# Sixteen rows of V instead of eight straight into the result, and a shorter serial stretch, at the end of a one-token attention kernel

## The chip, the cores and the metric

One core of one Trainium2 chip. The metric is the device time of one execution in microseconds (us), median of several executions. An execution's time is about 1.7 us longer than the span of its trace, so spans are compared with spans and times with times. The "granted clock" below is the share of TensorE's full clock that the trace shows: 1.00 is full, 0.50 half.

## The reference

```python
# q: [8, 32, 1, 128], k and v: [8, 32, 4096, 128], bf16
scores = jnp.einsum('bhqd,bhkd->bhqk', q, k) * 128 ** -0.5
attn = softmax(scores, axis=-1)
return jnp.einsum('bhqk,bhkd->bhqd', attn, v)
```

256 heads, one query each: every byte of K and V (537 MB) is read once.

## The kernel before

32 tiles of 8 heads. In a tile each of the 128 partitions holds C = 256 rows of 128 numbers ("row" below is one of these 256). VectorE and TensorE make the scores, ScalarE the weights `w`, TensorE the weighted sum of V. For the last three tiles four rows at a time are multiplied (a 128x512 matmul with 32 columns of weights), and the matmuls are dealt to four column groups of the array; each group sums into its own 32 partitions of `av` (these are the "value matmuls", and together the "value sum"). A copy to `comb` and four small matmuls with `pick` (the "sums over groups") bring these together in `op`; ScalarE scales `op` and stores it. The last rows of the last tile skip `av`: their weights, laid out in `w_last`, multiply V straight into `op` ("direct" matmuls, 128x128, 16 columns). The last V tile is loaded in seven pieces.

```python
LAST = 8
...
        ("v", NT - 1): [C // 2, C // 4, C // 8, C // 16, C // 32, LAST // 2, LAST // 2],
...
    def values_of(t, lo, hi):                      # cut
        end = C if t < NT - 1 else C - LAST
        group = [
            0 if t == NT - 1 and C // 2 <= c0 < C // 2 + 3 * C // 16 else c0 // CB % TG
            for c0 in range(0, end, CB)
        ]
        for c0 in range(lo, hi, CB):
            i = c0 // CB
            j = group[i]
            nc.tensor.matmul(                                                    # L322
                avs[t][j * AG : (j + 1) * AG, :], lhsT=w[:, i, :, :],
                rhs=vt[:, c0 : c0 + CB, :], start=(i < TG), stop=(j not in group[i + 1 :]),
            )
...
    def result_of(t):                              # cut; the copy to comb is L351
        if t == NT - 1:
            for i in range(LAST):
                nc.tensor.matmul(                                                # L361, direct
                    ops[n][:], lhsT=w_last[:, i, :], rhs=loads["v", t][:, C - LAST + i, :],
                    start=False, stop=False,
                )
        e = AG if t < LT else P
        for m in range(CB):
            nc.tensor.matmul(                                                    # L367, sum over groups
                ops[n][:], lhsT=pick[0:e, m, r, :], rhs=comb[0:e, m, :],
                start=(r == 0 and m == 0), stop=(r == R - 1 and m == CB - 1),
            )
...
        values_of(NT - 1, 0, C // 2)               # the end of the program
        norm_of(NQ - 1)
        recip_of(NQ - 1)
        values_of(NT - 1, C // 2, C - LAST)
        copy_of(NT - 1)
        result_of(NT - 1)
        finish_of(NQ - 1)                          # scaling, L376
        store_of(NQ - 1)
```

Of the kernel before, what the change touches and what calls it, by code (L numbers as in the profile page):

```python
# [15 lines left out]
TG = 4  # L16
R = 2
OB = 4
LAST = 8
LOOP = 6  # L20
EDGE = 2
NEG = -1.0e30
# [3 lines left out]
def kernel(  # L26
# [10 lines left out]
    P = nc.NUM_PARTITIONS  # L37
# [3 lines left out]
    C = S // PH  # L41
    NT = NH // G
# [4 lines left out]
    CB = 4  # L47
# [3 lines left out]
    AG = CB * G  # L51
    NV = C // CB
    assert (NV - 2 * EDGE) % LOOP == 0
    assert LAST % CB == 0 and TG * AG == P and NH % P == 0 and P % G == 0 and TB % PH == 0 and C % CB == 0

# [73 lines left out]

    w_last = consts.tile([P, LAST, RG], BF16, name="w_last")  # L130
    nc.gpsimd.memset(w_last[:], 0.0)
# [4 lines left out]
    def behind_loop(made):  # L136
# [10 lines left out]
        ("k", 0): [C // 4, C // 4, C // 2],  # L147
        ("k", NT - 2): [C // 2] * 2,
        ("k", NT - 1): [C // 4, C // 4, C // 2],
        ("v", NT - 1): [C // 2, C // 4, C // 8, C // 16, C // 32, LAST // 2, LAST // 2],  # L150
    }

    def load(kind, t):
# [78 lines left out]
    def weights_of(t):  # L232
# [26 lines left out]
        if t == NT - 1:  # L259
            for i in range(LAST // CB):  # L260
                nc.gpsimd.tensor_copy(
                    out=w_last[:, i * CB : (i + 1) * CB, RG - G : RG].rearrange("p m g -> p g m"),
                    in_=w[:, (C - LAST) // CB + i, :, :],
                )
# [40 lines left out]
    LT = NT - 3  # L305

    def values_of(t, lo, hi):
        vt = loads["v", t]
        w = ws[t]
        if lo == 0:  # L310
            avs[t] = ps_v.tile([P, CB * D], F32, name="av", tag="av")
        end = C if t < NT - 1 else C - LAST


        group = [
            0 if t == NT - 1 and C // 2 <= c0 < C // 2 + 3 * C // 16 else c0 // CB % TG
            for c0 in range(0, end, CB)
        ]
        for c0 in range(lo, hi, CB):
# [6 lines that stand above are left out]
# [28 lines left out]
    def result_of(t):  # L354
        n, r = divmod(t, R)
        comb = combs.pop(t)
        if r == 0:
            ops[n] = ps_o.tile([RG, D], F32, name="op", tag="op")
        if t == NT - 1:
            for i in range(LAST):  # L360
                nc.tensor.matmul(  # L361
                    ops[n][:], lhsT=w_last[:, i, :], rhs=loads["v", t][:, C - LAST + i, :],
                    start=False, stop=False,
                )
        e = AG if t < LT else P
        for m in range(CB):
            nc.tensor.matmul(  # L367
                ops[n][:], lhsT=pick[0:e, m, r, :], rhs=comb[0:e, m, :],
                start=(r == 0 and m == 0), stop=(r == R - 1 and m == CB - 1),
            )  # L370

    def finish_of(n):
        s, u = divmod(n, OB)
        if u == 0:
            stages[s] = o_pool.tile([RG, OB, D], BF16, name="stage", tag="stage")
        made = nc.scalar.activation(  # L376
            out=stages[s][:, u, :], in_=ops.pop(n)[:], func=ACT.Copy, scale=rzs.pop(n)[:, 0:1]
        )
        behind_loop(made)
# [12 lines left out]
    with tc.manual_schedule(engines={E.PE, E.DVE, E.Activation, E.SP}):  # L392
        q_prep(0)
        q_prep(1)
        for t in range(NT):
# [10 lines left out]
            if 0 < t - 1 <= LT:  # L406
                if (t - 1) % R == 0:
                    norm_of(n)
                if t > 1:
                    result_of(t - 2)  # L410
# [23 lines left out]
            if v_last:  # L434
                values_of(t - 1, 0, C)
# [4 lines left out]
            if t > 0:  # L440
                copy_of(t - 1)
                if t > 2 and t % R == 1:
                    store_of(n)
                if not loop:
                    if t % R == 0:
                        norm_of(n)
                    result_of(t - 1)
        values_of(NT - 1, 0, C // 2)
# [5 lines that stand above are left out]
        finish_of(NQ - 1)  # L454
        store_of(NQ - 1)
# [30 lines left out]
```

## Time and profile before

| | before |
|---|---|
| time, three runs | 1251.53, 1251.85, 1252.07 us |
| the execution whose trace was taken | 1252.91 us, span 1251.1 |
| HBM read | 536.94 MB, 429 GB/s over the span |
| busy: TensorE, VectorE, ScalarE | 63%, 82%, 13% |

The transfers are the bound until about 5 us before the end (39 of the page's 40 slices have the DMA engines busy for 90% or more, and the last piece of V lands at 1246.34 of 1251.1); what follows is the tail. The lines that carry this stand in the prediction.

### The profile page before, as it was taken

To read this page: it belongs to the slowest core of one execution; us is meant where nothing else is said; L and a number is where in the kernel's file an instruction comes from. 1 tells how busy PE (TensorE), PEld (TensorE's weight loads), DVE (VectorE), ACT (ScalarE), POOL (GpSimd) and SP (SyncE) were. 2 spreads that over 40 slices of the span, in tenths; PEclk is the share of its full clock that TensorE was granted. 3 is DMA by queue.
4 is the path that set the end of the run, shared out by engine and by line. 5 is a ranking of instruction groups with operands and counts; after the bars stand their busy time and mean duration, and the time that the engine had idled before them with its cause. 6 is when DMAs were issued, how large, how long until landed. Compare 5 with 4: busy or idle time off the path is not lost. (4 is left out here: it accounts for less than half of the span.)

```text
span 1251.1 us, 10828 instructions
## 1 busy us (share of the span) xinstructions
PE 794.4 (63%) x3110; PEld 301.4 (24%) x3110; DVE 1021.8 (82%) x495; ACT 166.1 (13%) x433; POOL 4.1 (0%) x22
## 2 busy tenths in 40 slices
PE   2466567655576655766557765577665776657756
PEld 0122122222232222322222222222222222212212
DVE  6977887878977789777798777987779877798783
ACT  0111011111011110111101111011110111101111
POOL 1000000000000000000000000000000000000000
PEclk9687788777887778877788877887877878779866
DMA  9999999999999999999999999999999999999997
GB/s 404 436 436 434 436 436 432 434 436 432 432 426 430 437 434 434 430 430 436 436 436 434 434 434 432 432 430 436 434 432 432 430 435 436 436 434 418 430 437 318
DMA packets 11432, 537.33 MB, mean 429 GB/s; under 512 B 1808, under 2 KB 2064, under 8 KB 2320
## 3 DMA queue, kind: packets, MB, share of 16 engines
q1 hardware_dynamic: 11072, 536.94, 99.4%
q8 instruction: 15, 0.25, 0.1%
q10 hardware_dynamic: 336, 0.07, 0.0%
q14 instruction: 9, 0.07, 0.0%
HBM read 536.94 MB, written 0.07 MB: 429 GB/s over the span
## 5 line engine op out<-in xcount | busy, mean ns | idle before, releaser
L191 DVE TENSOR_TENSOR kt<-kt,qb 128x8192 bf16<-128x8192 bf16 (+1 forms) x99 | 560.8, 5665 | 146.7 <-DMA kt<-in_k_dram 139.7
L211 PE MATMUL ps<-kt,ident 128*128 128x512 bf16 x800 | 284.1, 519 | 383.5 <-DVE kt L199 295.2
L294 PE MATMUL av<-vt,w 128*32 x1740 | 425.1, 396 | 4.6
L194 DVE TENSOR_TENSOR kt<-kt 128x4096 bf16<-128x4096 bf16 (+1 forms) x99 | 288.8, 2917 | 3.4
L294 PEld LDWEIGHTS av<-vt,w 128*32 x1740 | 173.0, 99 | 262.4 <-issue 120.1
L211 PEld LDWEIGHTS <-ident 128*128 128x128 bf16 x800 | 97.0, 121 | 563.9 <-issue 530.0
L223 DVE TENSOR_REDUCE sc<-ps 128x64 f32<-128x512 f32 x128 | 85.3, 685 | 53.4 <-PE ps L211 53.4
L248 ACT ACTIVATE e<-sc,nmax 128x256 bf16<-128x256 f32 x32 | 16.2, 508 | 705.9 <-DVE nmax L242 705.9
L255 ACT ACTIVATE w<-e,mine 128x256 bf16<-128x256 bf16 x256 | 105.6, 495 | 1.1
L199 DVE TENSOR_TENSOR kt<-kt 128x2048 bf16<-128x2048 bf16 x56 | 68.6, 1225 | 1.9
L351 ACT ACTIVATE comb<-av 32x512 bf16<-32x512 f32 (+1 forms) x32 | 18.8, 587 | 331.0 <-PEq L284 321.2
L280 PE MATMUL av<-vt,w 128*32 128x512 bf16 x116 | 47.1, 498 | 14.7 <-issue 13.2
L367 PE MATMUL op<-comb,pick 32*16 32x128 bf16 (+1 forms) x128 | 12.1, 213 | 22.1 <-ACT comb L351 22.1
L280 PEld LDWEIGHTS av<-vt,w 128*32 128x32 bf16 x116 | 6.9, 100 | 55.0 <-issue 55.0
L177 PE MATMUL qp<-qg,heads 8*128 8x128 bf16 x32 | 6.9, 216 | 16.8 <-ACT qg L175 16.8
L322 PE MATMUL av<-vt,w 128*32 128x512 bf16 x190 | 16.5, 425 | 0.7 <-DMA vt<-in_v_dram 0.7
L367 PEld LDWEIGHTS <-pick 32*16 32x16 bf16 (+1 forms) x128 | 8.7, 83 | 29.2 <-issue 28.8
L235 DVE TENSOR_REDUCE pmax<-sc 128x1 f32<-128x256 f32 x32 | 13.4, 420 | 1.1
L175 ACT ACTIVATE qg<-qh 8x128 bf16<-8x128 f32 x32 | 8.5, 267 | 33.7 <-PE qh L171 33.7
L171 PE MATMUL qh<-q_all,ident 128*8 128x128 bf16 x32 | 7.1, 223 | 8.9 <-DMA q_all<-in_q_dram 8.6
L179 ACT ACTIVATE qb<-qp 128x128 bf16<-128x128 f32 x32 | 8.9, 278 | 9.7 <-PE qp L177 9.7
L322 PEld LDWEIGHTS <-w 128*32 128x32 bf16 x190 | 6.9, 104 | 9.8 <-issue 5.8
(31 smaller groups left out, 48.1 us busy)
## 6 DMA issues: line engine op xcount, KB each, us to landing
kt<-in_k_dram SPq DMA_DIRECT2D x4, 4096.0 KB, 24.4
kt<-in_k_dram SPq DMA_DIRECT2D x4, 2048.0 KB, 13.4
vt<-in_v_dram SPq DMA_DIRECT2D x1, 4096.0 KB, 34.9
vt<-in_v_dram SPq DMA_DIRECT2D x1, 2048.0 KB, 39.4
vt<-in_v_dram SPq DMA_DIRECT2D x1, 1024.0 KB, 41.5
vt<-in_v_dram SPq DMA_DIRECT2D x1, 512.0 KB, 42.2
vt<-in_v_dram SPq DMA_DIRECT2D x31, 25.9
kt<-in_k_dram SPq DMA_DIRECT2D x29, 28.4
```

Of the source, the lines that this page charges most:

```text
L191: nc.vector.tensor_tensor(out=part, in0=part, in1=qb[:].to_broadcast([P, hi - lo, D]), op=ALU.mult)
L194: nc.vector.tensor_tensor(out=part[:, :, 0 : D // 2], in0=part[:, :, 0 : D // 2], in1=part[:, :, D // 2 : D], op=ALU.add,)
L199: nc.vector.tensor_tensor(out=part[:, :, 0 : D // 4], in0=part[:, :, 0 : D // 4], in1=part[:, :, D // 4 : D // 2], op=ALU.add,)
L211: nc.tensor.matmul(ps[:], lhsT=ident[:], rhs=kt[:, u * UC : (u + 1) * UC, s * DS : (s + 1) * DS], start=(s == 0), stop=(s == n - 1),)
L223: made = nc.vector.tensor_reduce(out=scs[t][:, u * UC : (u + 1) * UC], in_=sums.pop((t, u))[:], axis=AX.X, op=ALU.add)
L248: nc.scalar.activation(out=e[:], in_=sc[:], func=ACT.Exp, bias=nmax[:, 0:1], scale=scale, accum_out=esums[t // R][:, t % R : t % R + 1],)
L255: nc.scalar.activation(out=w[:, :, g, :], in_=e_g, func=ACT.Copy, scale=mine[:, 0, g : g + 1])
L280: pe.matmul(av, lhsT=wf[:, i * nw : (i + 1) * nw], rhs=vf[:, i * nv : (i + 1) * nv], **how)
L294: pe.matmul(av, lhsT=wf[:, bass.ds(ow + i * nw, nw)], rhs=vf[:, bass.ds(ov + i * nv, nv)], start=False, stop=False,)
L322: nc.tensor.matmul(avs[t][j * AG : (j + 1) * AG, :], lhsT=w[:, i, :, :], rhs=vt[:, c0 : c0 + CB, :], start=(i < TG), stop=(j not in group[ ...
L351: nc.scalar.activation(out=comb[0:n, :, :], in_=av[0:n, :, :], func=ACT.Copy)
L367: nc.tensor.matmul(ops[n][:], lhsT=pick[0:e, m, r, :], rhs=comb[0:e, m, :], start=(r == 0 and m == 0), stop=(r == R - 1 and m == CB - 1),)
```

## The change

Two edits. Rows 240-247 become direct too (16 direct rows instead of 8; the pieces of the load keep their sizes, 8, 4 and 4 rows, only their names change), and the last four direct matmuls go behind the sums over groups, so that they need not wait for the last piece before those. And only 24 rather than 48 rows, from row 128 on, are put in column group 0 alone.

```diff
-LAST = 8
+LAST = 16
@@
-        ("v", NT - 1): [C // 2, C // 4, C // 8, C // 16, C // 32, LAST // 2, LAST // 2],
+        ("v", NT - 1): [C // 2, C // 4, C // 8, C // 16, LAST // 2, LAST // 4, LAST // 4],
@@
-            0 if t == NT - 1 and C // 2 <= c0 < C // 2 + 3 * C // 16 else c0 // CB % TG
+            0 if t == NT - 1 and C // 2 <= c0 < C // 2 + 3 * C // 32 else c0 // CB % TG
@@ result_of (cut)
+        def last_rows(lo, hi):
+            for i in range(lo, hi):
+                nc.tensor.matmul(
+                    ops[n][:], lhsT=w_last[:, i, :], rhs=loads["v", t][:, C - LAST + i, :],
+                    start=False, stop=(i == LAST - 1),
+                )
+        if t == NT - 1:
+            last_rows(0, 3 * LAST // 4)
         for m in range(CB):
             nc.tensor.matmul(
                 ops[n][:], lhsT=pick[0:e, m, r, :], rhs=comb[0:e, m, :],
-                start=(r == 0 and m == 0), stop=(r == R - 1 and m == CB - 1),
+                start=(r == 0 and m == 0), stop=(r == R - 1 and m == CB - 1 and t < NT - 1),
             )
+        if t == NT - 1:
+            last_rows(3 * LAST // 4, LAST)
```

More of the change, by code (lines that the diff above doesn't have):

```diff
@@ L358, in result_of @@
             ops[n] = ps_o.tile([RG, D], F32, name="op", tag="op")
-        if t == NT - 1:
-            for i in range(LAST):
+        e = AG if t < LT else P
+        def last_rows(lo, hi):
+            for i in range(lo, hi):
                 nc.tensor.matmul(
                     ops[n][:], lhsT=w_last[:, i, :], rhs=loads["v", t][:, C - LAST + i, :],
-                    start=False, stop=False,
+                    start=False, stop=(i == LAST - 1),
                 )
-        e = AG if t < LT else P
+        if t == NT - 1:
+            last_rows(0, 3 * LAST // 4)
         for m in range(CB):
```

## The prediction

What no trace or run shows is cut from the text, and each cut is marked. Its sum comes to -1.07 us (scaling at 1247.36 instead of 1248.43), and the step of 1.0 behind 1250.85 is worked out from the trace of before. The 0.427, 0.218 and 0.056 us are times from start to start in that trace: 128x512 at half clock, 128x512 at full clock, 128x128 at full clock. That group 0 is a queue is read from those starts and the order of the program; the trace does not name a matmul's group.

> **What bounds the kernel now.** I read the page first (which resource is full), then the chain of waits that ended last (where the end is set), then the landings of the last V tile and the order of time over the last ten microseconds.
>
> The page:
>
> ```profile
> DMA  9999999999999999999999999999999999999997
> GB/s 404 436 436 434 436 436 432 434 436 432 432 426 430 437 434 434 430 430 436 436 436 434 434 434 432 432 430 436 434 432 432 430 435 436 436 434 418 430 437 318
> HBM read 536.94 MB, written 0.07 MB: 429 GB/s over the span
> ```
>
> Thirty-nine of forty slices are full of transfers at about 434 GB/s; only the last slice (31.3 us) falls, to 318. The change moves no byte, so it can only win in that tail. The chain that ended last shows the tail as links:
>
> ```profile
> 1201.87 39.43 DMA vt<-in_v_dram
> 1241.30 0.04 issue
> 1241.35 5.93 PE av L322 x26
> 1247.28 0.02 issue
> 1247.30 0.02 ACTq L351
> 1247.32 0.04 issue
> 1247.36 0.61 ACT comb L351
> 1247.97 0.04 issue
> 1248.01 0.40 PE op L367 x4
> 1248.41 0.02 issue
> 1248.43 0.36 ACT stage L376
> ```
>
> Up to 1241.30 the end waits for a V piece (rows 128 to 191 of each partition's 256; a "row" below is one of these 256); from then on for TensorE, then copy, sum over groups, scaling, store. The question is whether those 5.93 us of TensorE are held by data or by TensorE. The DMA view of the tail has issue to landing:
>
> ```profile
> vt<-in_v_dram SPq DMA_DIRECT2D x1, 1024.0 KB, 41.5
> vt<-in_v_dram SPq DMA_DIRECT2D x1, 512.0 KB, 42.2
> vt<-in_v_dram SPq DMA_DIRECT2D x1, 256.0 KB, 42.4
> vt<-in_v_dram SPq DMA_DIRECT2D x2, 128.0 KB, 29.2
> ```
>
> The issues start, by the order of time of the queue, at 1202.35, 1202.83, 1203.30, 1207.35 and 1226.69, so the pieces land at about: rows 192-223 at 1243.8, 224-239 at 1245.0, 240-247 at 1245.7, 248-251 at 1246.0, 252-255 at 1246.3 (the view of V's tile gives 19.6 us as the shortest landing, hence 1226.69 + 19.6 for the last, and 2 x 29.2 - 19.6 = 38.8 us for the other). The last value matmul starts at 1246.9, 1.2 us after its data. So TensorE is late, not the data, by about 0.9 us at the end. Busy time of TensorE in the throttle's own steps:
>
> ```profile
> 1238.76:1242.17 3.41, 2.70 (x24) 0.50 0.99 403
> 1242.17:1245.58 3.41, 3.41 (x16) 0.50 0.51 196
> 1245.58:1249.00 3.42, 2.50 (x33) 1.00 0.03 7
> ```
>
> (columns: length, TensorE busy, its matmuls, granted clock, DMA share, GB/s). The clock is half until 1245.58. And in the order of time the pace shows in the weight loads:
>
> ```profile
> 1244.71 0.15 PEld L322 LDWEIGHTS <-w 128*32 128x32 bf16 x1 [0.28 <-issue]
> 1245.14 0.15 PEld L322 LDWEIGHTS <-w 128*32 128x32 bf16 x4 [0.28 <-issue]
> 1245.57 1.19 PEld L322 LDWEIGHTS <-w 128*32 128x32 bf16 x16 [0.28 <-issue]
> 1247.09 0.61 PE L361 MATMUL op<-vt,w_last 128*16 128x128 bf16 x8
> ```
>
> From 1241.35 nine matmuls go one by one, 0.427 us apart; from 1245.14 four at a time. In the program 12 rounds (48 rows) are put in column group 0 alone, and of the 30 matmuls after 1241.35 group 0 gets 12 + 5 = 17, the other groups 5, 4 and 4. 17 explains the starts: ten at half clock, 1241.35 + 0.38 + 8 x 0.427 = 1245.14, one more step of 0.427 to 1245.57, then six steps of (1246.9 - 1245.57)/6 = 0.218 at full clock. Group 0 is thus a queue that never runs dry, and it alone ends the value sum; the other groups finish beside it.
>
> [...] 0.427 and 0.218 us, 0.056 us for the eight small ones ((0.61 - 0.219)/7), and the clock changes at the end of the window 1242.17 to 1245.58, the first after the wait that is wholly busy. [...] the program's last value matmul is in group 1, yet the one that starts last, at 1246.9, is by the count above group 0's 17th. [...] the copy starts 0.11 us after group 0's end (1246.875 + 0.379 = 1247.25). [...]
>
> **The change part by part.** The pieces keep their sizes (8, 4, 4 rows are now called LAST/2, LAST/4, LAST/4), so DMA is unchanged; comparing instruction order on each engine shows no move before the last tile. POOL makes four small copies of weights rather than two; the two took 0.46 us and were done at 1237.4, so four end near 1237.7, eight microseconds before use. Cost nil.
>
> *Removed:* the two value matmuls of rows 240-247, one of them group 0's last. *Moved:* rows 152-175 (six matmuls) are dealt to all groups. Group 0 now gets 6 + 5 = 11 matmuls: six alone (rows 128-148), then rows 160, 176, 192, 208, 224. The others get 5, 6 and 6. Group 0 keeps its pace: 11th start at 1241.35 + 0.38 + 9 x 0.427 = 1245.57. Do the waits hold? Its 9th (row 192) would start at 1244.71, data 1243.8; its 11th (row 224), data 1245.0. Both in time, the latter by 0.5 us. So its last start goes from 1246.88 to 1245.57, that is 6 x 0.218 = 1.31 us earlier. The end of the value sum is 1245.57 + 0.39 = 1245.96; the copy starts 0.11 later, 1246.07, takes 0.60, and the sum over groups may start 0.05 after it: 1246.71 instead of 1248.01.
>
> *Added beside:* twelve direct matmuls (rows 240-251), full clock by then. Eight from 1245.80 at 0.056: to 1246.24 (data 1245.7); four more to 1246.47 (data 1246.0). All under the copy, 0.24 us before it ends: nothing on the path.
>
> *Added on the path:* the four for rows 252-255 behind the four sums over groups: 4 x 0.056 = 0.22 us. Their data, 1246.3, is there before the sums start at 1246.71. So the last of eight starts at 1246.71 + 7 x 0.056 = 1247.10 and the scaling starts 0.256 later (as 1248.173 to 1248.429 now), at 1247.36 instead of 1248.43.
>
> Scaling, store and the closing semaphores (1248.43 to 1251.12, 2.69 us) are the same. Sum: -1.31 + 0.01 (a matmul across the clock's step) + 0.22 = -1.07 us in an execution with this clock phase: span 1250.0.
>
> **The clock's phase.** [...] I let its boundary B fall elsewhere. Before, with 17 x 0.427 = 7.25 us of cold work, half of what is left at B is saved: the value sum ends at about B + (7.25 - (B - 1241.35))/2. B = 1244.8: scaling starts near 1247.9 before, and 1247.0 after (now the landings at 1245.7 and 1246.0 hold the direct rows), gain 0.8. B = 1246.5: 1248.7 and 1247.6, gain 1.1. B = 1247.5: 1249.2 and 1248.1, gain 1.1. I take 1.0: 1251.85 - 1.0 = 1250.85.
>
> **Rivals.** (a) *A bigger gain*, 6 x 0.427 = 2.6 us, if the six serial matmuls counted at their cold length. Against: the last six steps of the queue are the warm ones, and ending earlier forgoes exactly those; besides, data land up to 1246.3. About 1249.3 even so. (b) *The clock stays at half.* [...] Against: group 0 alone still runs from 1241.35 to 1245.96, beyond 1245.58. (c) *A data wait replaces the queue.* If the last piece landed over 0.6 us later than here, the four matmuls behind would wait for it; a later landing of rows 224-239 moves everything. The end would gain less, some 0.5 us: 1251.3. (d) *All hidden, nothing gained*, as the load bounds the kernel: refuted by the 0.9 us between last landing and last value matmul's end.
>
> **Range and chances.** The three runs of before spread over 0.54 us, which the clock's phase alone can make, and the landings move with every execution. With a step of 1.0 from a 1251.85 base I take 1249.9 to 1251.7 for 8 in 10. Two per cent are 25 us; the whole tail behind the last landing is 4.8 us, so neither side is reachable by this change; 0.005 each for something unseen.
>
> **What would show it.** Right: L322 has 28 matmuls after the wait, singles for about 2.6 us less; the copy starts near 1246.1 (with full clock from about 1245.6) or 4.7 us after the wait's end; sixteen direct matmuls, twelve ending before the copy does; the scaling about 6.0 us after the wait's end, against 7.08 now. Wrong: an idle gap of TensorE with a V landing as its end ahead of row 224 or behind the sums; the clock at half beyond 1247; or the copy starting later than 0.11 us after group 0's last matmul.

## The result, and the profile after

1251.43 us median (1251.33 to 1251.86, 6 runs), against 1251.95 us (1251.53 to 1252.26, 6 runs) for the kernel before: 0.52 us. The ratio is 0.9997 with a 95% interval of 0.9984 to 1.001 (the ratios given here are not quite those of the medians quoted). The interval is 1.6 us wide to each side, more than any effect, so the gain in time is by itself not clear of noise; small differences are therefore read from the traces, and times are used where whole sets of runs stand apart.

Predicted was 1250.85, with 1249.9 to 1251.7 as range. The time is within it, and "within 2%" is right, but the gain is half of the 1.0 us predicted, and the range, 1.8 us wide, was met without the step that was to bring the gain, as the trace shows.

The trace after is from an execution of 1251.86 us, span 1250.2. The end of its chain of waits (start, length, what):

```profile
1204.55 41.43 DMA vt<-in_v_dram
1245.98 0.04 issue
1246.02 0.83 PE op L363 x12
1246.85 0.22 PE op L371 x4
1247.08 0.24 PE op L363 x4
1247.31 0.02 issue
1247.34 0.36 ACT stage L382
```

Before, the chain left the load at 1241.30, with the landing of rows 128-191, and spent 5.93 us in TensorE's value matmuls. Now it stays in the load until 1245.98: the issue at 1204.55 plus 41.43 us is the landing of rows 240-247 (the 256 KB piece). Behind it there are only the twelve direct matmuls, the sums, and the four direct ones. The copy is no link any more. The order of time shows what the value matmuls did meanwhile (in brackets: TensorE idle before, and what ended it):

```profile
1241.62 1.89 PE L322 MATMUL av<-vt,w 128*32 128x512 bf16 x16 [1.09 <-DMA vt<-in_v_dram]
...
1244.14 0.61 PE L322 MATMUL av<-vt,w 128*32 128x512 bf16 x8 [0.63 <-DMA vt<-in_v_dram]
...
1245.37 0.40 PE L322 MATMUL av<-vt,w 128*32 128x512 bf16 x4 [0.62 <-DMA vt<-in_v_dram]
...
1245.88 0.60 ACT L351 ACTIVATE comb<-av 128x512 bf16<-128x512 f32 x1 [7.59 <-PE av L322]
1246.02 0.83 PE L363 MATMUL op<-vt,w_last 128*16 128x128 bf16 x12 [0.25 <-DMA vt<-in_v_dram]
```

TensorE waits for each piece: 0.63, 0.62 and 0.25 us. The prediction had it late throughout. The reason is one column of the "windows", the stretches of 3.41 us at whose ends the granted clock changes in these traces (in the trace of before it falls at 675.56 and at 1238.76, 165 stretches of 3.413 us apart, and is back to full at 1245.58, two later). Here they are in the trace of after (length, TensorE busy, matmuls, clock, DMA share, GB/s):

```profile
1237.19:1240.60 3.41, 2.19 (x40) 1.00 0.96 405
1240.60:1244.01 3.41, 1.89 (x16) 1.00 0.87 344
1244.01:1247.43 3.42, 2.29 (x32) 1.00 0.21 76
```

The clock is full when rows 128-191 land; in the trace of before it was half until 1245.58. The program is the same up to there but for two more small copies on POOL, so the change did not cause this; *before_again* below shows the kernel before with full clock too. Two traces that differ in the clock cannot be subtracted: that scaling now starts at 1247.34 rather than 1248.43 is 1.09 us, almost exactly the predicted 1.07; the agreement is luck, for the larger part is not the change's doing.

### The profile page after: what moved, and what is told of

Same layout as the page of the kernel before. It is cut to its first block, busy times and chain, and to the rows that moved or that the text cites. A ratio compares the mean times of both kernels' runs of the same rounds, so it can differ in the third digit from the quotient of the medians. Undisturbed runs are those within 1.5% of the kernel's fastest.

```text
span 1250.2 us, 10842 instructions
## 1 busy us (share of the span) xinstructions
PE 786.8 (63%) x3116; PEld 299.6 (24%) x3116; DVE 1021.9 (82%) x495; ACT 166.1 (13%) x433; POOL 4.5 (0%) x24
## 5 line engine op out<-in xcount | busy, mean ns | idle before, releaser
L211 PE MATMUL ps<-kt,ident 128*128 128x512 bf16 x800 | 278.4, 511 | 389.9 <-DVE kt L199 299.7
L280 PE MATMUL av<-vt,w 128*32 128x512 bf16 x116 | 47.2, 499 | 14.6 <-issue 13.1
L322 PE MATMUL av<-vt,w 128*32 128x512 bf16 x188 | 13.7, 418 | 2.3 <-DMA vt<-in_v_dram 2.3
L237 DVE TENSOR_SCALAR spread<-same,pmax 128x32 f32<-128x32 f32 x32 | 7.7, 242 | 1.1
```

The source lines that it names most:

```text
L211: nc.tensor.matmul(ps[:], lhsT=ident[:], rhs=kt[:, u * UC : (u + 1) * UC, s * DS : (s + 1) * DS], start=(s == 0), stop=(s == n - 1),)
L280: pe.matmul(av, lhsT=wf[:, i * nw : (i + 1) * nw], rhs=vf[:, i * nv : (i + 1) * nv], **how)
L322: nc.tensor.matmul(avs[t][j * AG : (j + 1) * AG, :], lhsT=w[:, i, :, :], rhs=vt[:, c0 : c0 + CB, :], start=(i < TG), stop=(j not in group[ ...
```

## The experiments

Twelve runs. For each trace three things are compared: the clock at the landing of rows 128-191, and how long scaling starts after the last V piece (rows 252-255) and after rows 240-247 have landed. These delays do not depend on when the load ends, which moves by 0.4 us between executions. For the trace of before they are 2.09 and 2.76 us, for that of after 0.69 and 1.36; a table has them all. "Runs of before" are those made beside, on the same chip. Each expectation weighs two readings. The "clock theory" has the gain depend on whether the clock is half or full when rows 128-191 land; "corrected theory" adds that ordinary executions have full clock there.

**Full or half clock forced in both kernels.** For full clock, ten spare matmuls behind the second-last tile, where TensorE idled (cut; the 10 is written in):

```diff
+    def filler(n):
+        kt = loads["k", NT - 1]
+        ps = ps_s.tile([P, UC, DS], F32, name="fill", tag="ps")
+        for i in range(n):
+            nc.tensor.matmul(
+                ps[:], lhsT=ident[:], rhs=kt[:, 0:UC, 0:DS], start=(i == 0), stop=(i == n - 1)
+            )
@@
                 values_of(t - 1, 0, C)
+                if t == NT - 1:
+                    filler(10)
```

For half clock, 28 of the 32 matmuls of the last tile's first half left out; the result is then wrong (relative error 0.10):

```diff
         for c0 in range(lo, hi, CB):
             i = c0 // CB
+            if t == NT - 1 and TG <= i < C // 2 // CB:
+                continue
```

*before_warm*, the kernel before with the spare matmuls:

> The kernel before, with ten spare matmuls (128x512, 0.216 us each at full clock) on TensorE behind the second-last tile, where it idled for 2.5 us in the trace of before. Clock theory [...] the clock is full from about 1235 to the end, group 0's queue of 17 keeps up, and the tail is held by landings. From the landings of before, rows 240-247 at 1245.67: copy at about 1246.2, scaling 1247.3, about 0.9 us behind the last V landing (2.1 us behind it in the trace of before); time 0.5 to 1.0 us under before. Rival (landings come later in the changed kernel, clock is beside the point): time as before, 1251.95.

Measured: 1251.83 us (1251.74 to 1252.04), runs of before 1251.74 (1251.51 to 1252.03), ratio 1.0001 (0.9987 to 1.0015). Full clock from 1232.12 on; scaling 0.94 us after the last landing. The state of the tail was as expected, the time was not: the kernel before is not slower than its own copy with the clock held at full. So its ordinary runs lose nothing to the clock, and the traced one of 1252.91 us was the exception.

*after_warm*, the changed kernel with the same spare matmuls:

> The changed kernel with the same ten spare matmuls. Clock theory: full clock as in its own profile; scaling starts about 0.7 us behind the last V landing; only 0.2 to 0.3 us faster than the kernel before with the spare matmuls, since both wait for the same landings; and about as fast as the changed kernel's best (1251.3). Rival that the change itself costs or gains a fixed amount whatever the clock: the gap between the two is the 0.52 us of the pair without spare matmuls.

Measured: 1251.50 us (1251.41 to 1251.60), ratio to before 0.9998 (0.9984 to 1.0012). Scaling 0.70 us after the last landing. All five runs lie under all five of *before_warm*; the gap of the medians is 0.33 us, just above the expected 0.2 to 0.3.

*before_cold* and *after_cold*, with the 28 matmuls left out:

> The kernel before without 28 of the 32 matmuls of the first half of the last V tile (the result is wrong on purpose): TensorE idles from about 1235 to 1241.3 but for a few short ones. Clock theory: the clock is half when rows 128-191 land in every execution, group 0 has ten or so steps of 0.427 us, scaling starts 6.5 to 8.2 us after that landing (7.1 in the trace of before); time at or up to 0.5 us above before. Rival: time as before.

> The changed kernel with the same matmuls left out (wrong on purpose). Clock theory: half clock at the landing as above, group 0's 11 steps at 0.427 us, copy about 4.7 us after the landing, scaling 5.7 to 7.0 us after it; 0.8 to 1.1 us faster than the kernel before with the same left out. That is the step of 1.0 that I predicted for every execution. Rival (fixed amount): 0.52 us between the two.

Measured: *before_cold* 1252.53 us (1252.30 to 1253.38), ratio 1.0008 (0.9994 to 1.0022); *after_cold* 1251.58 us (1251.46 to 1252.29), ratio 1.0000 (0.9987 to 1.0014). The gap is 0.95 us; the two sets of runs do not overlap, though by 0.01 us only. Scaling 6.70 and 5.70 us after rows 128-191 landed. With half clock at that landing the change is worth about what I predicted for every execution, with full clock a third of that; a fixed 0.52 us fits neither gap. But the changed kernel does not get there as I had it. In the trace of *after_cold*, where the clock is full again at 1244.05 (at 1244.65 in that of *before_cold*), the copy starts 4.26 us after the landing, not 4.7, and scaling 1.36 us after rows 240-247, as at full clock: its group 0 has ended before rows 240-247 land, and the load sets the end.

**Ordinary executions, and each half of the change alone.**

*before_again*, no edit:

> The kernel before once more, unchanged. Its first trace came from an execution of 1252.91, a full microsecond above its timed median of 1251.85. Corrected theory: that execution was the exception and ordinary ones run the tail at full clock, as the kernel with spare matmuls did. Then a new profile most likely shows full clock from about 1242 on, scaling 0.9 to 1.0 us behind the last V landing (2.09 in the first trace) and a span near 1250.0; no timed run much above 1252.3. My first theory (half clock at the landing in nearly every execution): scaling 1.6 to 2.2 us behind the last landing again. Times within 0.15 of the runs of before beside it: the noise of the comparison.

Measured: 1251.72 us (1251.57 to 1252.13), runs of before 1251.80 (1251.52 to 1252.10), ratio 0.9999 (0.9985 to 1.0013). The windows of its trace, columns as above, below the window of the first trace that covers the same idle stretch:

```profile
1235.34:1238.76 3.42, 1.14 (x24) 1.00 0.95 405
...
1235.73:1239.15 3.42, 1.43 (x31) 1.00 1.00 426
1239.15:1242.56 3.41, 1.86 (x23) 1.00 0.96 387
```

and the end of its chain:

```profile
1203.52 42.27 DMA vt<-in_v_dram
1245.79 0.04 issue
1245.83 0.41 PE av L322 x2
...
1246.32 0.61 ACT comb L351
...
1246.97 0.40 PE op L367 x4
...
1247.39 0.36 ACT stage L376
```

Same kernel as the first trace, another execution. The window in which TensorE idles has 1.43 us of work here and 1.14 us there, because the windows lie elsewhere; there the clock fell to half, here it does not. And the chain has the shape of the changed kernel's: load until rows 240-247 land (1245.79), then 1.60 us of value matmuls, copy, sums, to scaling (0.94 after the last landing). Group 0's 17 matmuls, at 0.216 us, are no link.

*group_only* (the kernel before with `3 * C // 32` for `3 * C // 16`):

> Only the second half of the change: 24 rather than 48 rows in column group 0, the last 8 rows direct as before. Corrected theory: at full clock group 0's queue of 17 (0.216 us each, 3.7 us) ends before row 240 lands anyway, so ordinary executions gain nothing, within 0.15 us of before; scaling 0.9 to 1.0 us behind the last landing. If the shorter queue is where the 0.5 us of the change came from: 0.4 to 0.5 us under before.

Measured: 1251.82 us (1251.61 to 1252.33), ratio 1.0001 (0.9987 to 1.0015), nothing in time, as expected. By luck its trace has half clock, in almost the position of the first one:

```profile
1235.47:1238.88 3.41, 1.23 (x27) 1.00 0.99 418
1238.88:1242.30 3.42, 2.63 (x26) 0.50 0.98 397
1242.30:1245.71 3.41, 3.41 (x27) 0.50 0.47 181
```

```profile
1201.92 39.41 DMA vt<-in_v_dram
1241.33 0.04 issue
1241.37 4.90 PE av L322 x25
```

This is the pair that the trace of before needed: windows at 1238.88 and 1238.76, half clock in both, 4.90 instead of 5.93 us of value matmuls, scaling 1.05 instead of 2.09 us after the last landing. At half clock the shorter serial stretch alone saves 1.04 us after the landing; the expected 0.9 to 1.0 behind the last landing is missed by 0.05 only, although the clock was not the one that I had in mind. (This execution, at half clock, took 1251.82 us, the median of its kernel.)

*last_only* (the changed kernel with `3 * C // 16`):

> Only the first half of the change: 16 direct rows in three pieces, four of them behind the sums over groups, with 48 rows still in column group 0. Corrected theory: all of the ordinary gain is here, since the copy starts behind the landing of rows 224-239 rather than 240-247: 0.25 to 0.5 us under before, scaling 0.7 us behind the last landing, as in the changed kernel. If the queue of group 0 matters in ordinary executions: no gain, or less than half.

Measured: 1251.78 us (1251.38 to 1252.00), runs of before 1251.80, ratio 1.0000 (0.9986 to 1.0014). In time this is a miss: 0.02 us where 0.25 or more was expected. The trace shows the expected tail:

```profile
1203.38 42.26 DMA vt<-in_v_dram
1245.63 0.04 issue
1245.68 0.83 PE op L363 x12
1246.51 0.22 PE op L371 x4
1246.73 0.24 PE op L363 x4
```

Scaling 1.36 us after rows 240-247 and 0.69 after the last piece, with 48 rows still in group 0; the clock is half when rows 128-191 land and full from 1241.92, 0.62 us later. The traced execution is the fastest of the five (1251.38 us). They spread over 0.6 us, so an effect of 0.24 us can be lost in them; that the half alone gains it in time is not shown.

*all_ahead* (no direct matmuls behind the sums):

```diff
         if t == NT - 1:
-            last_rows(0, 3 * LAST // 4)
+            last_rows(0, LAST)
@@
-        if t == NT - 1:
-            last_rows(3 * LAST // 4, LAST)
```

(the `stop` flags moved back with them)

> The changed kernel with all 16 direct rows ahead of the sums over groups, none behind. In the trace of the changed kernel TensorE does 20 small matmuls without a gap from 0.04 us after rows 240-247 land, and the last piece lands 0.66 us after them, just as the twelfth ends. Theory: their order does not matter, within 0.1 us of the changed kernel, scaling 0.7 us behind the last landing. If the four behind hide the wait for the last piece: 0.1 to 0.3 us slower. If they lie on the path as I predicted (4 x 0.056): 0.2 faster.

Measured: 1251.62 us (1251.48 to 1251.82), ratio 0.9999 (0.9985 to 1.0013). Scaling 1.36 us after rows 240-247 and 0.69 after the last piece, the same to 0.01 us as with four behind. The order does not matter: 20 small matmuls follow the landing of rows 240-247 without a gap either way, and the last piece lands 0.66 us after it, when twelve have been started.

**The halves at half clock, and repeats.** The edits are those above together.

*before_cold2*, as *before_cold*:

> The kernel before with 28 matmuls left out, again, so that the half-clock variants are compared on one chip. About 0.8 us above the runs of before, as the first time (1252.53 against 1251.74).

Measured: 1252.93 us (1252.14 to 1253.82), runs of before 1251.84 (1251.68 to 1252.88), ratio 1.0010 (0.9997 to 1.0024); 1.09 us above, where 0.8 was expected. The five runs spread over 1.68 us. A likely reason is where the window ends at which the clock becomes full again: at 1244.65 in the trace of *before_cold* and 1245.69 here, with scaling 6.70 and 7.13 us after rows 128-191 landed.

*group_cold* (24 rows in group 0, 8 direct rows):

> Half clock forced, as before, by leaving out 28 matmuls of the last tile's first half (wrong result on purpose), with the shorter serial stretch (24 rows) alone, 8 direct rows. Theory: at half clock the queue of group 0 ends the value sum, so this half of the change carries the gain there: 12 steps rather than 17, until the landing of rows 240-247 takes over: 0.6 to 0.8 us faster than the kernel before with the same left out. If the direct rows carry the gain there too: nothing.

Measured: 1252.22 us (1251.83 to 1252.46), 0.71 us under *before_cold2*; ratio to before 1.0003 (0.9989 to 1.0017). Within 0.6 to 0.8, though the two sets of runs overlap; the traces have scaling 6.48 and 7.13 us after rows 128-191.

*last_cold* (48 rows in group 0, 16 direct rows):

> The same with the 16 direct rows alone and 48 rows still in column group 0 (wrong on purpose). Theory: the queue is 16 steps rather than 17 (0.22 us less), but four small matmuls go behind the sums (0.22 us more) and the twelve ahead queue behind group 0 too: within 0.2 us of the kernel before with the same left out. If the direct rows carry the gain at half clock too: 0.6 to 1.0 us faster.

Measured: 1253.22 us (1252.30 to 1254.17), ratio 1.0012 (0.9999 to 1.0026): 0.29 us above *before_cold2*, a little outside the expected 0.2, within the spread of both. The direct rows show no gain at half clock.

*after_again*, the changed kernel unchanged:

> The changed kernel once more, unchanged. Corrected theory: 0.25 to 0.5 us under the runs of before beside it; if the clock is half when rows 128-191 land, scaling is still under 1.3 us behind the last landing, at full clock 0.7.

Measured: 1251.73 us (1251.46 to 1251.92), runs of before 1251.84, ratio 0.9999 (0.9986 to 1.0013): 0.11 us, under the expected 0.25. In its trace the clock is half from 1238.26 to 1241.67 and full from then on, just after the landing at 1241.34; scaling 0.69 us after the last landing.

The traces together ("half clock": its last stretch in the tail; the other columns: from the landing to scaling):

| trace | half clock, us | after rows 240-247 | after the last piece |
|---|---|---|---|
| before | 1238.76 to 1245.58 | 2.76 | 2.09 |
| *before_cold* | 1237.83 to 1244.65 | 2.35 | 1.69 |
| *before_cold2* | 1238.87 to 1245.69 | 2.74 | 2.08 |
| *before_again*, *before_warm* | none | 1.60 | 0.94 |
| *group_only* | 1238.88 to 1245.71 | 1.72 | 1.05 |
| *group_cold* | 1239.68 to 1246.51 | 2.11 | 1.45 |
| *last_only* | 1238.50 to 1241.92 | 1.36 | 0.69 |
| *last_cold* | 1239.14 to 1245.97 | 3.00 | 2.33 |
| after, *all_ahead* | none | 1.36 | 0.69 |
| *after_warm* | none | 1.36 | 0.70 |
| *after_again* | 1238.26 to 1241.67 | 1.36 | 0.69 |
| *after_cold* | 1240.64 to 1244.05 | 1.36 | 0.69 |

Of the seven traces in which nothing was done to force the clock, four have half clock when rows 128-191 land. In two of these it is full again within 0.62 us, and nothing is lost. So half clock at the landing is not rare; half clock for three or four microseconds more is what costs the kernel before its time.

The kernel before has 38 runs with a median of 1251.79 us and one above 1252.4 (1252.88); the changed kernel has 11 with 1251.57. The difference, 0.22 us, agrees with the 0.24 us that the traces show at full clock (1.60 less 1.36). It mixes sessions, and the pairs alone gave 0.52 and 0.11. One part of the scatter lies behind everything compared here: from scaling to the end it is about 2.69 us in ten of the fourteen traces and 2.82 to 3.03 in the other four (after, *all_ahead*, *after_again*, *before_again*), as the store takes longer to land (1.3 us in the trace of before, 1.5 to 1.7 in these four). The prediction took the 2.69 us as fixed.

No variant was clearly faster than the changed kernel.

## Why the prediction was right or wrong

*Only the tail can gain, transfers and instruction order otherwise unchanged.* Right: 20 to 42 us from issue to landing for every piece as before, and the last slice of the page still the only one not full of transfers.

*Group 0 is a queue that ends the value sum; 17 steps become 11, -1.31 us; scaling 1.07 us earlier "in an execution with this clock phase".* Right in size where the clock stays half well past the landing: 1.04 us less from the last landing to scaling in *group_only* at the same phase, and 0.95 us in time between *before_cold* and *after_cold*. The two halves there go the way of the sum: the shorter stretch gives 0.71, the direct rows nothing. That the changed kernel's own 11 steps end the value sum is seen in no trace: in all five (with *all_ahead*) TensorE waits for rows 240-247. The sign "scaling about 6.0 us after the wait's end" came out at 5.76, the copy at 4.30 instead of 4.7.

*"The clock's phase".* This is the step that failed. I let the boundary B at which the clock recovers move from 1244.8 to 1247.5, and so assumed half clock for more than 3 us behind the landing in every execution; I took 1.0 us off the timed median 1251.85. What moves with the phase is also whether the clock falls at all, and whether it stays half for one window or two. TensorE idles before the last tile, for 2.53 us in the trace of before and 1.97 in that of after, and the windows cut this stretch differently (one starts at 1235.34 in the trace of before, at 1235.73 in that of *before_again*). The clock fell after a window with 0.47, 0.81, 1.14 or 1.23 us of work (*after_again*, *last_only*, before, *group_only*), and not with 1.43, 1.75 or 2.19 (*before_again*, *all_ahead*, after). It came back after one window in *after_again* and *last_only*, at 1241.67 and 1241.92, far below the 1244.8 with which I began. The kernel held at full clock is not faster than before (1251.83 and 1251.74), so most runs lose nothing to the clock. The gain worked out for an execution of 1252.91 us was taken from a median of executions that are mostly not like it. The numbers to notice this were there: the traced execution was slower than each timed one by about as much as the change was to save.

*What takes the term's place at full clock.* The queue takes 17 x 0.216 = 3.7 us (at full clock the last four value matmuls start at 1246.23, 1246.44, 1246.66 and 1246.88 in the trace of before), and is through with all that has landed by then when rows 240-247 land. The landing sets the start: from it to scaling 1.60 us before (*before_again*, *before_warm*), 1.36 with the 16 direct rows (six traces, see the table). Those 0.24 us come from the 16 direct rows, by *last_only*'s trace, though not by its times: the copy no longer waits for rows 240-247, and twenty small matmuls are shorter than two value matmuls, copy and four sums. It is the half of the change for which I had booked -0.22 and +0.22.

*Twelve direct matmuls "all under the copy, nothing on the path".* Wrong at full clock: the copy ended at 1246.48, the sums started at 1246.69, behind the twelfth. *Four behind the sums, 0.22 us on the path.* The length is right (0.24 in the chain), but *all_ahead* shows that nothing is lost or won by their place.

*Rivals.* (c), a data wait in the queue's place, is what happens in ordinary executions, though not for its reason: it asked for a last landing over 0.6 us later, and in the trace after it was 0.31 us later (0.12 in *before_again*); TensorE came sooner. Its figure, 1251.3, is nearer to 1251.43 than mine. Its sign, an idle gap of TensorE ended by a V landing ahead of row 224, is in the trace after. (a) and (b) did not occur. (d), nothing gained, is not excluded by the times of this pair; *after_warm*, whose runs all lie under those of *before_warm*, and the traces speak against it.

What stays open: the exact share of executions with half clock in the tail, since only mean clocks are known of runs without a trace, and why the changed kernel gained 0.52 us in one session and 0.11 in another; the medians of one kernel moved by up to 0.3 us between sessions. Open too is what decides whether a window's work is enough to keep the clock (see the last section).

## What to carry to other kernels

Before a trace's numbers are applied to a timed median, check that the traced execution lies among the timed ones; if it is off by as much as the change should save, the trace may show a state that the median does not. Where a granted clock differs between two traces, compare executions in the same clock state, or force the state in both kernels, before a difference is put down to the change. In a tail that is fed by pieces of a load, measure delays from the last landing, not from the start of the span.

## What the traces show of the clock, the starts and the landings

- In the tails of these traces windows with 1.14 and 1.23 us of work in 3.41 were followed by half clock, one with 1.43 was not. But TensorE's busy time alone does not tell them apart: earlier in the trace of before a window with 2.38 us (672.14 to 675.56, small matmuls for the most part) was followed by half clock, and one with 1.55 (1150.01 to 1153.42, 128x512 matmuls with 128 columns of weights) by full. Windows at half clock with 2.70 and 2.63 us were followed by another at half (before, *group_only*), one with 3.12 by full (*last_only*, 1238.50 to 1241.92), and so was one with 2.67 (before, 1156.84 to 1160.25). No limit comes out of these runs.
- In the trace of before nine value matmuls start one by one after 1241.35, 0.427 us apart, then four within 0.02 us at 1245.14, though in the program the first twelve are all group 0's. In the trace of after the first two start 0.22 us apart (1241.62 and 1241.84), then three within 0.01 us at 1242.06, though the first six are group 0's. The trace does not name the group of a matmul; that the ones that start together are of different groups, some of them ahead of their turn, is my reading of these starts, not shown. In the trace of before the copy started 0.11 us after the last value matmul ended (1247.25 and 1247.36).
- In the trace of before the sixteen landings of the last 128 KB piece ran from 1242.66 to 1246.34, 3.7 us. In the trace of after TensorE, which had idled for 0.25 us, started on rows 240-247 at 1246.02, 0.04 us behind the last of the sixteen landings of their piece (1245.98).
